# A chunked delta rule ahead of a SwiGLU block: the first pair of chunks solved with 16-row blocks and rounds u = v + N u, its loads reordered

## The chip, the cores and the metric

The kernel runs on one core of a Trainium2 chip. The metric is the device time of one execution in microseconds (us); lower is better. Five engines work side by side: TensorE (PE, matrix products into PSUM), VectorE (DVE), ScalarE (ACT), GpSimd (POOL) and SyncE (SP, which issues most loads and stores). Each takes its instructions in order.

## The reference

```python
# q, k, v: (4, 8, 768, 48); beta: (4, 8, 768); d_model 384, d_ff 1536; all float32
k_n = k / (norm(k, axis=-1) + 1e-6)
state = zeros((B, H, D, D))
for t in range(S):
    y[:, :, t] = einsum('bhd,bhde->bhe', q[:, :, t], state)
    v_old = einsum('bhde,bhd->bhe', state, k_n[:, :, t])
    state += beta[:, :, t] * outer(k_n[:, :, t], v[:, :, t] - v_old)
x = y.transpose(0, 2, 1, 3).reshape(3072, 384)
g = x @ w_gate
out = (g * sigmoid(g) * (x @ w_val)) @ w_out
```

The recurrence runs over 768 positions for each of 32 pairs of batch and head. The feed-forward network (FFN) then works on 3072 tokens.

## The kernel before

**Chunks.** The positions are cut into 12 chunks of 64 (`C`), two chunks to a group. Within a chunk the recurrence becomes a triangular system: with the strictly lower part L of diag(beta) K K^T, the updates u of all 64 positions are u = (I + L)^-1 diag(beta) (v - K state). `gram` makes the products K K^T and Q K^T on PE, `mask_q` cuts the latter to its triangle into `p_sb`. `invert` makes the inverse's diagonal blocks of 32 rows (`R`) for both chunks of a group and all heads at once: 128 partitions hold 4 blocks of 32 rows, the free dimension holds 32 x 32 elements. `substitute` runs it on DVE, 31 steps of one product (`tmp`, L524) and one addition (`zb`, L530), each step waiting for the one before. The block below the diagonal is then joined on PE (`join`, for the first two groups `join_late` with its helpers `late_z` and `d_o`), and the transposed inverse lies in `ztp`.

**One chunk's steps.** `advance(c)` is a generator with four or five steps: K state and Q state (p_r, p_y), u by the inverse (p_u, copied to `uu`), the new state (p_s) and y (p_y), then y turned by PE (p_f) into the FFN's input `x_ffn`.

**The FFN.** `gate_val(c, f)` makes 2 x 128 columns of gate and of value for the 256 tokens of chunk c (24 passes of PE at L1052; a float32 product is two passes in the profile), Silu on ACT and the product of both on DVE. From chunk 2 on a form with fewer products is used (`gate_val_fast`, L957, and `output_fast`, L1160). Between their products, `point` puts steps of the next chunks into PE's queue, and `fill` puts weight conversions or substitution steps into DVE's.

**Weights.** The 36 pieces of weights are staged by SP as raw words (`stage`, L250) into tiles that are free at that time, and `convert` brings each into its place with two activations on ACT (`power_step`, L262 and L268) and three instructions on DVE (L279, L287, L299). Pieces 0 to 11 hold 256 columns each (128 x 2 KB), pieces 12 to 23 hold 512; the last 12 are rows of `moe_w_out`. A place is staged again when its piece has been converted (`freed_by`). `need(n)` converts up to piece n before the products that read it.

**The order** is written out by hand for all engines (`manual_schedule`); the code's order is each queue's order. It begins with K of chunks 0 and 1 (SP and ACT queues), beta (POOL and SP), norms of K (POOL's power, L368), then four weight pieces, Q of chunk 0, K of chunks 2 and 3, six weight pieces, V of chunk 0, Q of chunk 1 and more weights. K, Q and V come in rows of 48 elements (192 bytes), four or eight loads to a chunk. The first group has its own order: `first_gram`, `first_diag` (diagonal blocks, L566), `first_below`, `first_scale` (L579 to L582), the 31 steps, `late_z`, two joins, and conversions of 12 pieces in between:

```python
        for n, _ in enumerate(substitute(mb, zb)):
            if n == R // 2:
                for i in range(4):
                    power_step(i)
        m_1 = turned_m(1, "ffn")
        scale_v_heads(0)
        turned(1, True, "px")
        for _ in late_z(0, zb):
            pass
```

After that the FFN of chunk 0 starts, with chunk 1's steps between its products. `turned_m` (L602) turns group 1's blocks on PE for its later inverse.

Of the kernel before, what the change touches and what calls it, by code (L numbers as in the profile page):

```python
# [13 lines left out]
C = 64  # L14
# [6 lines left out]
def kernel(  # L21
# [108 lines left out]
    def halves(x, c, bp, b):  # L130
        return x[2 * bp + b, :, c * C : (c + 1) * C, :]

    def load_k(c, dmas=(nc.sync,)):
        for n in range(2 * NB):
            bp, b = divmod(n, 2)
            dmas[n % len(dmas)].dma_start(
                out=kn_of(c)[64 * b : 64 * b + 64, bp, :, 0:D],
                in_=halves(k, c, bp, b).rearrange("h p d -> p h d"),
            )

    def load_q(c):
        for bp in range(NB):
            for b in range(2):
                nc.sync.dma_start(
                    out=qpad[c % QB][64 * b : 64 * b + 64, bp, :, 0:D],
                    in_=halves(q, c, bp, b).rearrange("h p d -> p h d"),
                )
# [28 lines left out]
    def load_v(c):  # L176
        vin[c] = work.tile([128, 2, NB, NJ, D], FP32, name="vin", bufs=2)
        for bp in range(NB):
            for b in range(2):
                src = halves(v, c, bp, b).rearrange("(j par) p d -> par p j d", par=2)  # L180
                for par in range(2):
                    s = 64 * (b ^ par)
                    nc.sync.dma_start(out=vin[c][s : s + 64, par, bp], in_=src[par])
# [11 lines left out]
    for f0, m in ((0, 256), (256, 256), (512, PIECE), (1024, PIECE)):  # L195
        for t in range(KT):
            for dst, src in ((wg_sb, moe_w_gate), (wv_sb, moe_w_val)):
                pieces.append((dst, src, t, f0, m))
# [22 lines left out]
    place_of += in_wo + in_z1 + in_wo + in_work + (in_z1 + in_work) * 3  # L221

    beta_s = places["wo"].bitcast(FP32)[:, 6 * H_ : 6 * H_ + NG * 128]
    LATE = {"zb": 0, "p_sb": 6}
# [13 lines left out]
    def stage(n):  # L238
# [11 lines left out]
        nc.sync.dma_start(  # L250
# [3 lines left out]
    def power_step(n):  # L254
# [3 lines left out]
        power = words(hp[10 + (n // 2 % 4 if n < N_HALF else (0, 2, 3, 1)[n % 4])])  # L258
# [11 lines left out]
    def convert(ns):  # L270
# [24 lines left out]
        for n in range(ns[-1] + 1, ns[-1] + 7):  # L295
            if n < min(N_HALF, len(pieces)) or ns[-1] + 3 > n < len(pieces):
                power_step(n)
# [15 lines left out]
    for b in range(2):  # L313
        rows = mask_q[64 * b : 64 * b + 64]
        nc.gpsimd.affine_select(
            out=rows,
            in_=rows,
            compare_op=ALU.is_ge,
            fill=0.0,
            base=-1,  # L320
            pattern=[[1, C]],
            channel_multiplier=-1,
        )

# [51 lines left out]
    def load_beta(at, queue=nc.gpsimd):  # L376
# [5 lines left out]
            in_=beta.rearrange("(bp b) (j par) s -> b par bp j s", b=2, par=2)[  # L382
# [13 lines left out]
    def scale_v_heads(c):  # L396
        r = vin[c].rearrange("p par bp j d -> p (par bp j) d")
        for h in range(HH):
            nc.scalar.mul(r[:, h], r[:, h], n_t[c // 2][:, c % 2, h : h + 1])

    scaled = set()

    def scale_v(c):
        scaled.add(c)
        spent.append(1.4)
        r = vin[c].rearrange("p par bp j d -> p (par bp j) d")
        n = n_t[c // 2][:, c % 2, :, None].to_broadcast([128, HH, D])
        nc.vector.tensor_tensor(out=r, in0=r, in1=n, op=ALU.mult)

    def banks(name, tag):  # L410

        if tag == "ffn":
            return [ps_ffn([128, 512], name) for _ in range(2)]
# [3 lines left out]
    def turned(c, of_q, tag=None):  # L417

        tag = tag or ("py" if of_q else "px")
# [5 lines left out]
        if c >= blocks_of[of_q][1]:  # L425
            xt_v = xt.rearrange("p (bp b j i) -> p bp j b i", bp=NB, b=2, j=NJ)
# [19 lines left out]
    def gram_steps(c, of_q, tag=None, copies=(nc.vector.tensor_copy,) * 2):  # L446

        xt = (qt if of_q else kt)[c]
        p_g = banks("p_g", tag or ("py" if of_q else "px"))
# [47 lines left out]
    z1s, mbs = {}, []  # L497
    WAIT = "wait"
# [40 lines left out]
    first_of = {}  # L539

    def first_tiles():
        a = work.tile([128, C * 2 * HH], FP32, name="a_sb")

        first_of["flat"] = a[:, 0 : R * R]
        first_of["diag"] = a[:, 0 : R * R].rearrange("p (j h) -> p h j", j=R)
        a_sb[0] = a[:, R * R :].rearrange("p (c h j) -> p c h j", c=2, h=HH)
        zb = work.tile([128, R, R], FP32, name="zb", bufs=1)
        nc.vector.memset(zb, 0.0)
        nc.vector.memset(ztp[0], 0.0)
        first_of["zb"] = zb  # L550

    def first_gram(c, tag):
# [9 lines left out]
        return p_g, p_v  # L562

    def first_diag(c, par, p, copy):
        at = HH * c + HH // 2 * par
        copy(first_of["diag"][:, at : at + HH // 2], p[1][:, par, 1])  # L566

    def first_below(c, p):
        for lo in (slice(R, C), slice(64 + R, 64 + C)):
            nc.scalar.copy(  # L570
                a_sb[0][lo, c].rearrange("p (par h) j -> p par (h j)", par=2),
                p[0][lo, :, 0 : HH // 2 * R],
            )

    def first_scale(mb, r_b):
        zb, b = first_of["zb"], beta_b[:, 0]
        nb = work.tile([128, R], FP32, name="nb", tag="nb_1", bufs=1)
        for _ in range(2):
            nc.gpsimd.tensor_tensor(out=b, in0=b, in1=r_b, op=ALU.mult)  # L579
        nc.gpsimd.tensor_copy(zb.rearrange("p k i -> p (k i)")[:, 0 : R * R : R + 1], b)  # L580
        nc.vector.tensor_scalar_mul(nb, b, -1.0)
        nc.vector.tensor_tensor(  # L582
            out=mb, in0=mb, in1=nb[:, None, :].to_broadcast([128, R, R]), op=ALU.mult
        )
        return zb
# [7 lines left out]

    def turned_m(g, tag):

        a_v = a_of[g].rearrange("p (m i) -> p m i", i=C)
        p_m = banks("p_m", tag)
        half_r = R // 2
        for j in range(R):
            p = p_m[j // half_r][:, R * (j % half_r) : R * (j % half_r) + R]  # L600
            for quad, at in QUADS:
                nc.tensor.matmul(p[quad], a_v[quad, :, at + j], ident[quad, quad])  # L602
        return [
            (slice(half_r * n, half_r * n + half_r), p.rearrange("p (j i) -> p j i", i=R))
            for n, p in enumerate(p_m)
        ]
# [50 lines left out]
    def invert(g):  # L657
# [3 lines left out]
        if g > 1:  # L661
            mb = new_mb()
            yield from turn(mb.rearrange("p j i -> p i j"), a_v[:, R:C])
        else:
            mb = mbs.pop()
# [82 lines left out]
    def advance(c):  # L748
# [7 lines left out]
        p_y = recur(ps_pair("p_y", "py"))  # L756
        if c > 0:
            p_r = recur(ps_pair("p_r", "px"))
# [20 lines left out]
        yield  # L779
        p_u = recur(ps_pair("p_u", "px"))  # L780
        for bp, j, par, b, first in every():
# [8 lines left out]
        uu = work.tile([128, 2, NB, NJ, D], FP32, name="uu", tag="r", bufs=2)  # L790
        each = range(NB) if c == 0 else (slice(0, NB),)
        for bp in each:
            nc.scalar.copy(uu[:, :, bp], p_u[:, :, bp])
# [6 lines left out]
        pq = p_sb.pop(c)  # L800

        def p_of_u():
            for bp, j, par, b, first in every():
# [4 lines left out]
                    start=(c == 0 and first),  # L808
# [29 lines left out]
        p_of_u()  # L838
        y = work.tile([128, NB, NJ, 2, D], FP32, name="y", tag="r", bufs=2)
        for bp in each:  # L840
            nc.scalar.copy(y[:, bp, :, 0], p_y[:, 0, bp])
            for b in range(2):
                nc.scalar.copy(y[half_of(b), bp, :, 1], p_y[half_of(1 - b), 1, bp])
# [201 lines left out]
    def gate_val(c, f, fill, within=None):  # L1045

        ps = {}
        for w_sb, name in ((wg_sb, "p_gate"), (wv_sb, "p_val")):
# [11 lines left out]
            if name == "p_gate":  # L1060
                nc.scalar.activation(sil, ps[name], ACTF.Silu)
                fill(2)
                if within is not None:
                    point(within)
        new_h(c, f, len(hs))
        nc.vector.tensor_tensor(out=hs[c, f], in0=sil, in1=ps["p_val"], op=ALU.mult)
        fill(3)
# [24 lines left out]
    def store(c, bp, o_sb):  # L1092
        for b in range(2):
            nc.sync.dma_start(
                out=out_v[2 * bp + b, c * C : (c + 1) * C],
# [166 lines left out]

    gens = {}

    def step(kind, fn, *args):
# [3 lines left out]
        next(gens[key][0], None)  # L1269
        gens[key][1] += 1  # L1270
# [22 lines left out]
    first = []  # L1293
# [13 lines left out]
    def may_advance(c):  # L1307
        g = c // 2
        due = {0: 1, 1: 2 + 2 * (c % 2)}.get(g, 2)
# [13 lines left out]
    def prep_step(c):  # L1323

        if first:
            first.pop(0)()
            return True
# [46 lines left out]
    def fill(n):  # L1374
        if todo:

            filled.append(n)
            converts(2 if len(filled) < 4 else 1)
            if len(filled) == 1:
                converts(1)  # L1380
# [17 lines left out]
    with tc.manual_schedule(  # L1398
# [9 lines left out]
        for at in range(0, 16, 2):  # L1408
            load_beta(at)
            load_beta(at + 1, nc.sync)  # L1410
# [3 lines left out]
        nc.vector.memset(places[0][:, 0:1], 0)  # L1414
        norms(1)
        for n in range(4):
            stage(n)
# [3 lines left out]
        for n in range(4, 10):  # L1421
            stage(n)
        load_v(0)
        load_q(1)
        stage(10)
        stage(11)
        copy_a, copy_v = nc.scalar.copy, nc.vector.tensor_copy
        turned(0, False)
# [8 lines left out]
        mb = new_mb()  # L1437
        nc.vector.transpose(
            mb.rearrange("p j i -> p (j i)"), first_of["flat"]
        )  # L1440
        for n in range(12, 17):
            stage(n)
        load_v(1)
        zb = first_scale(mb, r_b)
        for c in range(2):
            first_below(c, p_g[c])

        turned(0, True, "ffn")
        turned(2, False, "px")
        turned(3, False, "py")  # L1450
        first_q = gram_steps(0, True, "ffn")
        next(first_q)
        gram(2, False, "px", (copy_a, copy_a))
        gram(3, False, "py", (copy_a, copy_a))
        for n, _ in enumerate(substitute(mb, zb)):
            if n == R // 2:
                for i in range(4):
                    power_step(i)
        m_1 = turned_m(1, "ffn")
        scale_v_heads(0)  # L1460
# [101 lines left out]
```

## Time and profile before

| | us |
|---|---|
| median of 3 runs (713.03 to 714.13) | 713.82 |
| the profiled execution, time | 713.96 |
| its span, first to last instruction | 712.3 |
| PE busy | 679.6 |
| DVE busy | 475.6 |
| ACT busy | 261.8 |
| POOL busy | 53.8 |

A row of the profile's groups names the line, engine and operation, then output and inputs with shapes. Busy times of different engines overlap. The chain of waits goes back from the last instruction: at each step to what released it, or to the instruction before it on its engine, so its pieces add up to the span. The granted clock is the share of full speed at which PE was allowed to run.

### The profile page before, as it was taken

What the parts mean: (1) busy time and instruction counts of PE and PEld (TensorE: products, weight loads), DVE (VectorE), ACT (ScalarE), POOL (GpSimd) and SP (SyncE); (2) the same over time, 40 slices, a digit from 0 to 9 for tenths busy, and PEclk for the clock granted to TensorE, in tenths of its full rate; (3) what the DMA queues carried; (4) which work ended last, traced back from release to release, by engine and by line L of the source; (5) the groups of instructions that cost most, each with busy time, mean ns of one, the idle gap of its engine ahead of it and who ended that gap; (6) DMA issues with size and microseconds to landing.
All of it is one profiled execution on the core that took longest, in us unless ns stands there. A gap on an engine that the chain in (4) does not pass through costs nothing.

```text
span 712.3 us, 25668 instructions
## 1 busy us (share of the span) xinstructions
PE 679.6 (95%) x11368; PEld 637.9 (90%) x11368; DVE 475.6 (67%) x1085; ACT 261.8 (37%) x555; POOL 53.8 (8%) x46
## 2 busy tenths in 40 slices
PE   4747999999999999999999999999999999999997
PEld 3636788866799999999999999999999999999997
DVE  5995765779799967888458888469854345333342
ACT  3557755312453343224333235233153043142230
POOL 8003000201300030000120000300000000000000
PEclk9556999999999999999999999999999999999999
DMA  7786444002753162166144166035142142121210
GB/s 149 173 230 171 128 112 131 26 12 45 206 111 80 40 119 67 26 136 133 29 97 105 25 125 123 18 97 113 24 112 71 24 99 60 47 68 46 67 46 22
DMA packets 144575, 62.57 MB, mean 88 GB/s; under 512 B 124400, under 2 KB 127472, under 8 KB 144464
## 3 DMA queue, kind: packets, MB, share of 16 engines
q1 hardware_dynamic: 141968, 60.36, 36.1%
q8 instruction: 89, 1.46, 0.8%
q10 hardware_dynamic: 2112, 0.39, 0.4%
q0 software_dynamic: 384, 0.17, 0.1%
q14 instruction: 22, 0.18, 0.1%
HBM read 53.82 MB, written 7.08 MB: 86 GB/s over the span
## 4 chain that ended last, share of the span: by engine, by line
PE 89%; DVE 5%; ACT 3%; issue 1%; DMA 1%; SPq 0%; DVEq 0%; ACTq 0%
PE ffn L957 42%; PE ffn L1160 19%; PE ffn L1052 9%; PE ffn L1077 4%; PE p_g L452 3%; PE p_s L816 2%; PE p_r L760 2%; PE p_u L782 2%; DVE tmp L524 2%; DVE zb L530 2%; PE p_y L769 1%; PE p_y L804 1%; PE p_f L853 1%; DMA kn<-in_k_dram 1%; PE p_j L723 1%
## 5 line engine op out<-in xcount | busy, mean ns | idle before, releaser
L957 PE MATMUL ffn<-x_ffn,wg_sb 128*128 128x128 f32 x840 | 128.3, 275 | 0.4 <-ACT x_ffn L856 0.2
L957 PE MATMUL ffn<-x_ffn,wv_sb 128*128 128x128 f32 x840 | 128.1, 275 | 0.0
L957 PEld LDWEIGHTS ffn<-x_ffn,wg_sb 128*128 128x128 f32 x840 | 111.1, 192 | 0.7 <-ACT ffn L1013 0.3
L957 PEld LDWEIGHTS ffn<-x_ffn,wv_sb 128*128 128x128 f32 x840 | 110.7, 192 | 0.0
L987 ACT ACTIVATE sil<-ffn 128x256 f32<-128x256 f32 x120 | 46.0, 383 | 131.9 <-PE ffn L957 126.8
L1160 PE MATMUL ffn<-wo_sb,h_f 128*128 128x192 f32 x480 | 83.4, 327 | 0.0
L992 DVE TENSOR_TENSOR h_f<-sil,ffn 128x256 f32<-128x256 f32 x120 | 49.6, 418 | 47.6 <-ACT sil L987 45.1
L1160 PEld LDWEIGHTS ffn<-wo_sb,h_f 128*128 128x128 f32 x480 | 78.1, 190 | 0.4
L1121 DVE TENSOR_TENSOR ffn<-ffn,p_sb 128x512 f32<-128x512 f32 x58 | 40.4, 696 | 44.6 <-ACT ffn L1013 43.5
L530 DVE TENSOR_TENSOR zb<-zb,tmp 128x31 f32<-128x31 f32 (+15 forms) x186 | 63.7, 343 | 6.4
L524 DVE TENSOR_TENSOR tmp<-zb,mb 128x31 f32<-128x31 f32 (+15 forms) x186 | 63.2, 340 | 5.2
L957 PE MATMUL ffn<-x_t,h_f 128*128 128x128 f32 x480 | 61.2, 280 | 0.1
L957 PEld LDWEIGHTS ffn<-x_t,h_f 128*128 128x128 f32 x480 | 56.2, 191 | 1.4 <-ACT ffn L970 0.3
L668 POOL TENSOR_TENSOR n_b<-mb,half 128x32 f32<-128x32 f32 x5 | 30.0, 5995 | 297.6 <-DVE mb L494 258.5
L1121 DVE TENSOR_TENSOR o_sb<-o_sb,ffn 128x192 f32<-128x192 f32 x49 | 17.2, 351 | 51.2 <-PE ffn L1160 49.1
L970 ACT COPY ffn<-ffn 128x512 f32<-128x512 f32 x30 | 17.1, 571 | 63.6 <-PE ffn L957 57.2
L1052 PE MATMUL ffn<-x_ffn,wg_sb 128*128 128x256 f32 x144 | 35.8, 401 | 0.9 <-ACT x_ffn L856 0.9
L1160 PE MATMUL ffn<-last_k,h_f 128*128 128x192 f32 x200 | 35.9, 327 | 0.0
L1052 PE MATMUL ffn<-x_ffn,wv_sb 128*128 128x256 f32 x144 | 33.4, 381 | 0.0
L1052 PEld LDWEIGHTS ffn<-x_ffn,wg_sb 128*128 128x128 f32 x144 | 28.3, 201 | 5.6 <-ACT x_ffn L856 1.4
L1160 PEld LDWEIGHTS ffn<-last_k,h_f 128*128 128x128 f32 x200 | 32.9, 190 | 0.0
L1052 PEld LDWEIGHTS ffn<-x_ffn,wv_sb 128*128 128x128 f32 x144 | 27.0, 190 | 3.7
(242 smaller groups left out, 1048.1 us busy)
## 6 DMA issues: line engine op xcount, KB each, us to landing
h_f<-w_s SPq DMA_DIRECT2D x60, 256.0 KB
p_sb<-w_s SPq DMA_DIRECT2D x27, 256.0 KB
vin<-in_v_dram SPq DMA_DIRECT2D x96, 48.0 KB
out_dram<-o_sb SPq DMA_DIRECT2D x48, 96.0 KB
kn<-in_k_dram SPq DMA_DIRECT2D x40, 96.0 KB
zt<-in_moe_w_out_dram SPq DMA_DIRECT2D x6, 384.0 KB
qpad<-in_q_dram SPq DMA_DIRECT2D x36, 64.0 KB
wo_sb<-in_moe_w_gate_dram SPq DMA_DIRECT2D x4, 512.0 KB
```

The costliest lines, as they stand in the source:

```text
L452: nc.tensor.matmul(p_v[par][half_of(b if of_q else b ^ par), bp, j], kt[c][half_of(par), bp, j, b], xt[half_of(par), bp, j, b],)
L524: nc.vector.tensor_tensor(out=t_v, in0=zb[:, 0 : j + 1, j : j + 1].to_broadcast([128, j + 1, m]), in1=mb[:, j : j + 1, j + 1 : R].to_broad ...
L530: nc.vector.tensor_tensor(out=zb[:, 0 : j + 1, j + 1 : R], in0=zb[:, 0 : j + 1, j + 1 : R], in1=t_v, op=ALU.add,)
L668: nc.gpsimd.tensor_tensor(out=n, in0=mb.rearrange("p j i -> p (j i)")[:, 0 : R * R : R + 1], in1=half, op=ALU.pow,)
L957: nc.tensor.matmul(p[:, u], w(u), moving, start=start and u == 0, stop=True, skip_group_check=True,)
L970: nc.scalar.copy(p_y, p_x)
L987: nc.scalar.activation(sil[:, n].rearrange("p (i n) -> p i n", i=2), p[:, 0:2], ACTF.Silu)
L992: nc.vector.tensor_tensor(out=h_of(c, f, j), in0=sil[:, n].rearrange("p (i n) -> p i n", i=2), in1=p[:, 2:4], op=ALU.mult,)
L1052: nc.tensor.matmul(ps[name][:, i], w_sb[:, t, (f + i) * 128 : (f + i + 1) * 128], xts[c][:, t], start=(t == 0 and i == 0), stop=(t == KT - 1),
L1077: nc.tensor.matmul(p_o, hs[c, f - f % 2][:, f % 2, bp * 128 : (bp + 1) * 128], wo_sb[:, f], start=(f == 0), stop=(f == FT - 1),)
L1121: nc.vector.tensor_tensor(out=out, in0=a, in1=b, op=ALU.add)
L1160: nc.tensor.matmul(p[x, part], a(f - f % 2)[:, f % 2], b(f), start=not begun and f == 0, stop=f == FH - 1, skip_group_check=True,)
```

## The change

- The first group uses diagonal blocks of 16 rows: 15 steps on two blocks per partition (`first_substitution`) for the 31 steps on one.
- Instead of joining blocks, N = -Z L is made on PE (`n_products`, from the blocks below the diagonal in `l_sb` and the block inverse in `ztp[0]`), then v0 = Z r, and three rounds u = v0 + N u. With four blocks of 16 rows, N^4 is zero, so three rounds are exact. For chunk 0 the halves of each round (`par`) lie in PSUM tiles of their own and one weight piece is converted behind each half's addition.
- The joins, `turned_m` and the scaling of v by heads on ACT go; v of chunks 0 and 1 is scaled on DVE. The Gram product of Q and K of chunk 1 comes ahead of the FFN.
- Loads: K and Q of a chunk in two transfers, V in four; K and Q of chunks 0 to 3 and V of chunk 0 ahead of all weights; four of the beta loads on ACT's queue. The batches are assigned to the halves of the partitions the other way, in loads and stores.
- Weight columns 512 to 1023 come in pieces of 256, so there are 42 pieces; six are converted before the FFN starts, where it were twelve.
- 100 one-column products into PSUM that nothing reads, ahead of the first transposes.
- In chunk 0's first two gate blocks a step of `advance` and one or two conversions follow each quarter of the products.

```diff
+    def load_heads(t, x, c, dmas=(nc.sync,)):
+        for b in range(2):
+            dmas[b % len(dmas)].dma_start(
+                out=t[64 * b : 64 * b + 64, :, :, 0:D].rearrange("p bp h d -> p (bp h) d"),
+                in_=halves(x, c, b).rearrange("bp h p d -> p (bp h) d"),
+            )
...
-    for f0, m in ((0, 256), (256, 256), (512, PIECE), (1024, PIECE)):
+    for f0, m in ((0, 256), (256, 256), (512, 256), (768, 256), (1024, PIECE)):
...
+    def unread():
+        p = ps_pair("p_t", "px")[:, 0]
+        for n in range(100):
+            q_ = QUADS[n % 4][0]
+            nc.tensor.matmul(p[q_, 0:1], ident[q_, q_], ident[q_, 0:1])
...
+    def first_substitution():
+        zb, mb = pairs_of_blocks(first_of["zb"]), pairs_of_blocks(first_of["mb"])
+        for j in range(B16 - 1):
+            m = B16 - 1 - j
+            shape = [128, 2, m, j + 1]
...
+            nc.vector.tensor_tensor(
+                out=t_v, in0=zb[:, :, j : j + 1, 0 : j + 1].to_broadcast(shape),
+                in1=m_v.to_broadcast(shape), op=ALU.mult,
+            )
+            nc.vector.tensor_tensor(out=z_v, in0=z_v, in1=t_v, op=ALU.add)
...
+    def n_products(c, p_n, pars):
...
+                nc.tensor.matmul(
+                    p_v[par][half_of(b), bp, j], l_sb[c][rows, h], zt[rows, h]
+                )
...
     def advance(c):
...
+        if c < 2:
+            yield MORE
+            uu = new_u("uu")
+            p_n = single(2) if c == 0 else [p_u[:, par] for par in range(2)]
+            for n in range(3):
+                for par in by_par(p_n, n_sb[c], uu if n else v0, 0, True):
+                    if c == 0:
+                        plus(uu[:, par], v0[:, par], p_n[par])
+                        if n + par < 3:
+                            yield MORE
+                if c > 0:
+                    plus(uu, v0, p_u)
+                    if n < 2:
+                        yield MORE
...
-            load_beta(at + 1, nc.sync)
+            load_beta(at + 1, nc.sync if at % 4 else nc.scalar)
...
-        for n in range(4):
-            stage(n)
         load_q(0)
         load_k(2)
         load_k(3)
-        for n in range(4, 10):
+        load_q(1)
+        load_v(0)
+        for n in range(12):
             stage(n)
-        load_v(0)
-        load_q(1)
-        stage(10)
-        stage(11)
+        load_v(1)
+        stage(12)
+        stage(13)
...
+        unread()
         turned(0, False)
         turned(1, False, "py")
...
+        first_substitution()
+        for n in range(14, 18):
+            stage(n)
+        first_z()
+        for n in range(18, 23):
+            stage(n)
+        some, others = slice(0, HH // 2), slice(HH // 2, HH)
+        spread_z(0, 1, nc.scalar, some)
+        spread_z(0, 0, nc.vector)
+        spread_z(0, 1, nc.vector, others)
+        scale_v(0)
...
+        step("advance", advance, 0)
+        power_step(0)
+        power_step(2)
...
+        for n in (0, 2, 4, 1, 3, 5):
+            step("advance", advance, 0)
+            converts_first(n)
+        step("advance", advance, 0)
+        p_n = banks("p_n", "px")
+        n_products(1, p_n, (0,))
+        step("advance", advance, 0)
+        n_products(1, p_n, (1,))
+        scale_v(1)
...
+        def chain(at):
+            step("advance", advance, 0 if steps("advance", 0) < 4 else 1)
+            converts(1 + (at + 1) % 2)
```

`first_z` transposes the block inverse (1024 elements); `spread_z` copies it with a mask into `ztp[0]`, for half the rows each time; `low_copies` brings the blocks below the diagonal from PSUM to `l_sb` on ACT, 12 copies for both chunks; `n_copy` brings N from PSUM to SBUF on ACT.

## The prediction

> **What bounds the kernel now.** I read the page first, then the busy time by stretch, then the chain of waits of the first 80 us, then the order of VectorE's (DVE's) instructions. The page says that TensorE (PE) is the bound, but not in the first slices:
>
> ```profile
> PE 679.6 (95%) x11368; PEld 637.9 (90%) x11368; DVE 475.6 (67%) x1085; ACT 261.8 (37%) x555; POOL 53.8 (8%) x46
> ...
> PE   4747999999999999999999999999999999999997
> ...
> PEclk9556999999999999999999999999999999999999
> ```
>
> In the table by stretch (columns: PE, weight loads, DVE, ACT, POOL busy, clock granted to PE, DMA share, GB/s) the bound changes hands at about 80 us: until 60 DVE is busy nine tenths and PE idles at half clock, afterwards PE is full.
>
> ```profile
> 30.00:40.00 10.00, 4.32 (x256) 3.92 (x256) 9.21 (x24) 7.59 (x27) 0.00 (x0) 0.63 0.68 175
> ...
> 50.00:60.00 10.00, 6.00 (x189) 5.06 (x180) 8.64 (x29) 9.66 (x26) 3.26 (x1) 0.50 0.54 118
> 60.00:70.00 10.00, 9.05 (x150) 7.26 (x151) 4.02 (x8) 5.65 (x11) 2.37 (x1) 0.66 0.69 195
> ...
> 80.00:90.00 10.00, 10.00 (x224) 8.56 (x223) 7.01 (x11) 5.15 (x10) 0.00 (x0) 1.00 0.05 14
> ```
>
> The chain says what fills the opening (start, length, what): 31 substitution steps of two DVE instructions, then transposes, a join and its copies, then the first FFN product at 62.37, at half clock (5.03 against 2.80 us for the same 12), and a last hole that ends at 78.54.
>
> ```profile
> 20.34 0.20 DVE tmp L524
> ...
> 21.87 0.28 DVE tmp L524
> ...
> 59.87 1.55 PE p_f L853 x6
> ...
> 62.37 5.03 PE ffn L1052 x12
> 67.40 1.08 PE p_s L816 x64
> 68.48 0.68 PE ffn L634 x50
> 69.16 2.80 PE ffn L1052 x12
> ...
> 77.91 0.58 ACT zt L654
> ...
> 78.54 1.16 PE p_g L452 x64
> ```
>
> So the span is F, the start of the first FFN product, plus the PE work behind it, plus PE's losses there. Before: F = 62.4. From 78.54 on PE is full: 712.3 - 78.5 = 633.8. Between F and 78.54 PE did 12 + 12 FFN passes (5.6 at full clock), L816 (1.1), L634 (0.7) and most of L646 (1.9): 9.3 us of work in 16.2, so 6.9 were lost, 2.2 of it to the clock. Work behind F: 633.8 + 9.3 = 643.1.
>
> **Part 1, up to the substitution (ends at 20.3 before).** POOL's two powers (L368, 6.50 us from 9.20) end at 15.7, and add, reciprocal and transpose bring r_b at 16.6. These stay. Behind them the change needs the last diagonal copy (0.59), the 1024-element transpose (1.25), nb (0.14) and a scaling of 512 elements instead of 1024 (0.65 for 1.23): 19.3, if the diagonal is there. The diagonal may be the later one: four beta loads now sit in ACT's queue ahead of the first K copies, at the 0.61 us that one beta load costs SP, and they wait for earlier loads, so I put those copies at 10 rather than 7.5. PE then reaches the second Gram block at 12.5; before, it stood from 12.7 to 15.4 in an "issue" gap between records, so there is room, and I take 19.3 to 20.3, middle 19.8. The new zero fills, mask sums and products of m_rows are small DVE work ahead of 6.38, where DVE waited for K anyway; without that cover they would cost about 1 us.
>
> **The 100 unread products** (1 column each, two passes) run before K lands. The Gram products, as small, did about 208 passes from 9.84 to 12.53: 12.9 ns each. 200 passes are 2.6 us, from 2.1 to 4.7; K's first chunk starts its DVE work at 6.38, so they cost nothing. The Trainium skill ("TensorE: Matmul & The Clock Gate", "Wait — 56ns, not 53.3ns?") speaks against it: no start-to-start below about 25 ns, and 62 ns where firmware decodes. That is an estimate of 5.0 us (end at 7.1, 0.7 late) or 12.4 (end at 14.5, some 7 late). The measured 12.9 ns is already under that floor, as four quadrants take turns, so I take it. Nor do I see a gain: the clock row shows 9 for the first slice already, it falls to half at about 15.6, right behind PE's gap, 11 us after these products are done, and no stage before then is set by PE. Bounds -1 and +7, value 0.
>
> **Part 2, the substitution.** The old steps fit 0.195 us + 1.05 ns per element, start to start (31 elements 0.23, 112 elements 0.31); the fit gives 23.5 for the measured 23.4. The new one has 15 steps x 2 instructions over 1360 elements of each kind: 30 x 0.195 + 2720 x 0.00105 = 8.7 us. Saved 14.6. It ends at 28.5.
>
> **Part 3, from there to F (18.7 us before).** What goes: the transposes L610 and L616 (1.92 + 1.21), the join's copies (1.30 + 0.38 + 2.36), two copies of m (0.59 each) and six pairs of weight pieces in between; the 16 scalings of v on ACT (3.70) become one of DVE. What comes, on DVE: transpose 1.2 (L616 1.21), two spreads of 512 and 256 (0.65 + 0.4, from L582), the scaling of v (0.95, as L356), four masked copies (2.6, L470 1.29 for two): 34.3. PE meanwhile at half clock: 64 passes of N (2.2) and 64 of p_u (2.0; L804 took 1.96) from 30.8 give 35.0; ACT's copies of N (0.6 each) fit, if ACT is free by then: from 16.9 it has 12 copies of the blocks below the diagonal (5.8, by L570's 0.59 for 512 elements), 8 of K and Q (4.3) and 4 of Gram blocks (2.2), to 29.2, and its first spread comes at 29.7; 0.5 of cover, and what exceeds it delays F. The halves of v0 (0.6) are there at 35.6. Six half rounds follow. Their PE part (32 passes, 1.0) hides behind DVE, whose own sequence is one addition of 384 elements from PSUM (0.56, between 192 elements in 0.351 and 512 in 0.696) and one weight piece (0.29 + 0.42 + 0.42 + 0.1 of gaps = 1.23, when it stands alone): 1.83. First addition done at 35.6 + 1.0 + 0.7 = 37.3, the sixth at 46.4. Then p_y's second half 1.0, y copies 0.7, p_f 1.55, x copies 0.9 and gaps 0.2: F = 50.8, against 62.4: 11.6 earlier. The separate PSUM tiles are what lets one half's products run while the other half is added; without it each half round would be 1.0 longer, 6 us in all.
>
> **Part 4, behind F.** PE work: three rounds for chunk 1 (3 x 1.08) are added; its join (0.68 + 1.94) goes, and one Gram block (1.16) has moved ahead of F: -0.5, so 642.6. Losses: the cold clock again, 2.2. Only 6 weight pieces are converted at F, 12 before, and the second gate block needs 12, the third 18, the fourth 24. DVE up to there: 18 pieces at 0.86 (paired) to 1.23, about 19 (6 pieces of 512 columns are now 12 of 256: 1.72 a pair for some 1.6, nothing), and additions, state and h 8: 27 us. PE up to there: 30.6. DVE has about 4 us of cover, but ACT holds two pieces' activations (0.66 a piece) ahead of a copy that PE needs (about 1 us), and the fourth block waits for the last three pieces (about 1). 4.5 lost by this schedule, 6.9 in the old; I take 6.
>
> **The loads.** SP, ACT and POOL issue the same first loads; SP is moved past Q0, K2, K3, Q1, V0 (about 2 MB in 192-byte rows) before the first weights. Issue costs per load hardly depend on size (0.61 for 48 KB, 0.63 to 0.71 for 96 KB), so half as many loads issue faster, and the rows then run at the 130 to 200 GB/s of 2 to 8 us and 16 to 24 us: 10 to 15 us from about 8.5, when the second K chunk has landed. Six pieces (1.6 MB at the 350 GB/s of 24 to 28 us) then land by 23 to 28; ACT first reads one at 35. Cover 7 us or more; without it F moves one for one. K4 and the pieces behind it on SP wait for p_s at F + 4 and are needed at F + 22 and later.
>
> Sum: 50.8 + 642.6 + 6 = 699.4, and 1.66 outside the span (713.96 - 712.3): 701.1. The profiled run is 0.1 above the median of 713.82, so I say 701.0.
>
> **Rivals.**
> 1. A warmer clock. Before, one dense stretch at 26 to 29 bought 3.4 us of full clock. If the denser rounds do the same, N, p_u, p_y, p_f and the first gate products save 2.0 + 0.5 + 0.9 + 2.2, about 6: 695. Against: PE is only about half busy in the rounds, and at 6.00 of 10 us (50 to 60) the clock stayed at 0.50.
> 2. PE waits for its own instructions or for landings. It stood in "issue" gaps of 2.7 and up to 3.9 us (L560, L602) while loads ran; one such gap ahead of N and one near F: 705.
> 3. Slower than before: the weight pieces become the bound behind F. From 62.4 to 71.1 DVE finished three pieces of double size, idle in between for ACT, which waited for pieces not staged (SP queue held by PE and DVE). At that 2.9 us for each of 18 pieces the fourth gate block starts at F + 52 instead of F + 35 (1.9 a piece with all else): 718. It turns the sign from F + 48 on, 2.7 us a piece. Against: pieces 6 to 22 are staged before F.
> 4. The 100 products cost the estimate's long end, 7 us: 708. Against: the 12.9 ns.
>
> **How the numbers follow.** Forecast 0.60 (its own range 697 to 706), rival 1 0.16, rival 2 0.14, rival 4 0.03, rival 3 0.06, and 0.01 for one that ends at no change. 694 to 708 leaves out rival 3 and the tails. A change under 0.2% (1.4 us) can't be told from none: faster 0.93, same 0.01, slower 0.06.
>
> **What would show it.** Substitution rows 30 in 8.7 us, starting at 19 to 20; additions about 1.8 us apart; first FFN product at 49 to 53, at half clock; PE full from about F + 36. Wrong if additions lie over 2.5 us apart, if PE waits for a landing of a weight piece, or if the stretch F to F + 40 shows PE under 8 of 10.

## The result, and the profile after

The changed kernel takes 709.26 us (median of 5 runs, 706.98 to 710.56), and the kernel before, beside it on the same chip, 714.13 (713.03 to 715.15): a ratio of 0.9932, with a 95% interval of 0.9909 to 0.9956. The change gains 4.9 us, where the forecast was a gain of 13. The profiled execution took 709.14 with a span of 707.4, against a forecast span of 699.4. So 8.0 us are to be explained: F, the start of the first FFN product, came at 53.4 instead of 50.8, and the part behind it took 654.0 instead of 648.6.

The page of the changed kernel, first rows (busy time, then TensorE and its clock in 40 slices, then the queue that carries instructions: packets, MB, share):

```profile
PE 683.2 (97%) x11440; PEld 643.0 (91%) x11440; DVE 473.6 (67%) x1092; ACT 261.8 (37%) x548; POOL 52.9 (7%) x46
...
PE   6689999999999999999999999999999999999997
...
PEclk9799999999999999999999999999999999999999
...
q8 instruction: 90, 1.47, 0.9%
```

PE was busy for 679.6 us before and is so for 683.2 now; 2.8 of the 3.6 more are the unread products. The clock row has lost its stretch of fives. The last row is one that the prediction did not read: 1.47 MB in 90 packets are 16 KB a packet.

The stretches that the prediction showed; 30 to 40 is where it had put the N products (columns: PE, weight loads, DVE, ACT, POOL, clock granted to PE, DMA share, GB/s):

```profile
30.00:40.00 10.00, 4.87 (x179) 4.62 (x178) 4.57 (x8) 3.54 (x9) 0.00 (x0) 0.83 0.88 241
50.00:60.00 10.00, 9.77 (x288) 8.13 (x284) 3.95 (x11) 6.47 (x17) 0.00 (x0) 1.00 0.44 81
60.00:70.00 10.00, 9.49 (x211) 7.98 (x210) 6.52 (x16) 7.41 (x21) 0.00 (x0) 1.00 0.10 26
80.00:90.00 10.00, 9.55 (x166) 8.10 (x166) 6.09 (x20) 7.86 (x17) 0.00 (x0) 1.00 0.66 216
```

From 50 on PE is full and warm, as hoped. But from 30 to 40 every engine in the row is idle for more than half of the time. The chain of waits of the changed kernel tells what stood there (start, length, what):

```profile
29.44 0.52 PE ffn L458 x33
29.95 4.41 issue
34.36 1.02 PE ffn L458 x28
...
35.49 1.71 PE p_n L667 x62
...
40.62 0.04 DVE uu L1260
...
42.21 0.55 DVE uu L1260
...
48.56 0.56 DVE uu L1260
...
53.46 0.63 PE ffn L1189 x2
```

PE stops in the middle of Q1's Gram products, after 33 passes, and the row names no other engine that it waited for. That its next instructions were missing is what experiments 4 to 7 and 11 go into. The N products, queued behind, begin at 35.1 instead of 31. The six additions (L1260) are then 1.6 us apart.

### The profile page after: what moved, and what is told of

Read it like the earlier page. It is cut to its first block, busy times and chain, and to the rows that moved or that the text cites. A ratio compares the mean times of both kernels' runs of the same rounds, so it can differ in the third digit from the quotient of the medians.

```text
span 707.4 us, 25711 instructions
## 1 busy us (share of the span) xinstructions
PE 683.2 (97%) x11440; PEld 643.0 (91%) x11440; DVE 473.6 (67%) x1092; ACT 261.8 (37%) x548; POOL 52.9 (7%) x46
## 3 DMA queue, kind: packets, MB, share of 16 engines
q8 instruction: 90, 1.47, 0.9%
## 4 chain that ended last, share of the span: by engine, by line
PE 91%; DVE 3%; ACT 2%; issue 2%; DMA 1%; SPq 0%; DVEq 0%; ACTq 0%
PE ffn L1093 42%; PE ffn L1299 19%; PE ffn L1189 8%; PE ffn L1216 4%; PE p_g L458 3%; PE p_u L876 2%; PE p_s L944 2%; PE p_r L838 2%; PE p_y L932 1%; PE p_y L847 1%; DMA kn<-in_k_dram 1%; PE p_f L989 1%; PE p_u L896 1%; PE p_t L444 1%; PE p_j L801 1%
## 5 line engine op out<-in xcount | busy, mean ns | idle before, releaser
L1093 PEld LDWEIGHTS ffn<-x_ffn,wg_sb 128*128 128x128 f32 x840 | 111.1, 192 | 0.7 <-ACT ffn L1149 0.3
L1260 DVE TENSOR_TENSOR ffn<-ffn,p_sb 128x512 f32<-128x512 f32 x58 | 40.4, 697 | 44.3 <-ACT ffn L1149 43.2
L536 DVE TENSOR_TENSOR zb<-zb,tmp 128x31 f32<-128x31 f32 (+15 forms) x155 | 53.1, 343 | 5.3
L530 DVE TENSOR_TENSOR tmp<-zb,mb 128x31 f32<-128x31 f32 (+15 forms) x155 | 52.7, 340 | 4.0
L1260 DVE TENSOR_TENSOR o_sb<-o_sb,ffn 128x192 f32<-128x192 f32 x49 | 17.2, 352 | 51.2 <-PE ffn L1299 49.1
L1189 PE MATMUL ffn<-x_ffn,wg_sb 128*128 128x256 f32 x144 | 34.3, 384 | 0.0
L1093 PE MATMUL ffn<-x_ffn,p_sb 128*128 128x128 f32 x216 | 30.3, 283 | 0.5 <-issue 0.5
```

The source lines that it names most:

```text
L530: nc.vector.tensor_tensor(out=t_v, in0=zb[:, 0 : j + 1, j : j + 1].to_broadcast([128, j + 1, m]), in1=mb[:, j : j + 1, j + 1 : R].to_broad ...
L536: nc.vector.tensor_tensor(out=zb[:, 0 : j + 1, j + 1 : R], in0=zb[:, 0 : j + 1, j + 1 : R], in1=t_v, op=ALU.add,)
L1093: nc.tensor.matmul(p[:, u], w(u), moving, start=start and u == 0, stop=True, skip_group_check=True,)
L1189: nc.tensor.matmul(ps[name][:, i], w_sb[:, t, (f + i) * 128 : (f + i + 1) * 128], xts[c][:, t], start=(t == 0 and i == 0), stop=(t == KT - 1),
L1260: nc.vector.tensor_tensor(out=out, in0=a, in1=b, op=ALU.add)
```

## The experiments

Each was timed beside the kernel before. "F" and "behind F" are of the profiled execution.

| kernel | median us (range) | ratio to before (95%) | F | behind F |
|---|---|---|---|---|
| the change | 709.26 (706.98 to 710.56) | 0.9932 (0.9909 to 0.9956) | 53.4 | 654.0 |
| 1: no unread products | 705.28 (705.13 to 708.72) | 0.9881 (0.9866 to 0.9897) | 52.4 | 651.5 |
| 2: chunk 1's rounds on four quadrants | 706.24 (705.84 to 708.97) | 0.9897 (0.9882 to 0.9911) | 53.0 | 651.2 |
| 3: same order, two quadrants | 708.6 (706.65 to 708.98) | 0.9913 (0.9900 to 0.9925) | 54.4 | 652.9 |
| 4: some weights later | 709.32 (705.40 to 711.47) | 0.9917 (0.9890 to 0.9943) | 53.0 | 654.5 |
| 5: 64 unread products | 706.73 (704.20 to 708.91) | 0.9907 (0.9894 to 0.9921) | 50.7 | 651.8 |
| 6: 36 unread products | 706.71 (705.20 to 708.71) | 0.9901 (0.9886 to 0.9916) | 50.8 | 653.9 |
| 7: 128 unread products | 712.28 (708.67 to 713.40) | 0.9963 (0.9951 to 0.9975) | 59.1 | 651.3 |
| 8: as 1 and 4 together | 707.26 (705.92 to 709.41) | 0.9908 (0.9894 to 0.9922) | 56.4 | 651.2 |
| 9: loads paced | 709.20 (706.65 to 713.08) | 0.9933 (0.9908 to 0.9958) | 51.5 | 653.5 |
| 10: as 1 and 9 together | 706.50 (705.54 to 707.14) | 0.9889 (0.9876 to 0.9902) | 54.0 | 651.3 |
| 11: 36 unread products behind F | 710.70 (708.93 to 711.42) | 0.9939 (0.9926 to 0.9951) | 55.0 | 654.7 |

Two habits help with this table. The part behind F repeats well: experiments 1, 5, 7, 8 and 10, which will turn out to be alike there, give 651.2 to 651.8. F does not: less the 651.5 behind it, the five spans of experiment 1 (703.4 to 707.0) give an F from 51.9 to 55.5. Experiment 11 executes the same instructions as 1 up to F, and its profile has F 2.6 us later. So F of one profile is one draw, and for what happens ahead of F the medians are the measure.

**1. Without the unread products.** The call is left out.

```diff
-        unread()
```

> The changed kernel without its 100 unread products. Theory A (they do nothing for the time): PE's granted clock in 27 to 60 us stays at full speed as in the changed kernel, the first FFN product starts within 1.5 us of 53.5 apart from where PE's gaps of its own instructions fall (400 records fewer, so the gap of 4.4 us at 30 us moves), and the time lies at 706 to 710. Theory B (they keep the clock up for the first stage): the clock falls to half in most of 10 to 50 us as it did before the change, the first FFN products take 0.42 us a pass instead of 0.25, the first FFN product starts 2 to 4 us later, and the time is 711 to 714.

The median fell to 705.28, 4 us under the change, with intervals that do not touch. It lies under the ranges of both theories. Theory B is right in part, as the opening has more of the half clock without the products: granted at half from 16.9 to 23.7 and from 33.9 to 44.2 us, against 20.8 to 27.6 and 34.4 to 37.8 in the change. But the kernel is faster all the same, and its first six FFN passes take 1.49 us, at full clock, as in the change.

The products' own time is not the reason, for in the change they ran at about the speed that the prediction took from the Gram products (14.2 ns a pass against 12.9). The start of PE's timeline of the changed kernel:

```profile
1.90 2.84 PE L582 MATMUL p_t<-ident 32*32 32x1 f32 x200 [1.90 <-POOL ident masks.py:199]
5.85 1.94 PE L444 MATMUL p_t<-ident,kn 128*128 128x128 f32 x8 [1.11 <-DMA kn<-in_k_dram]
```

200 passes from 1.90 to 4.74, and then PE waits for K anyway. The Trainium skill's floors of 25 or 62 ns ("TensorE: Matmul & The Clock Gate", "Wait — 56ns, not 53.3ns?") did not hold for them, and yet the products were not free. What they take is not time but places: 100 products are 400 instructions (two passes, each with its weight load). Experiments 5 to 7 and 11 follow that.

**2 and 3. Chunk 1's rounds.** They took 2.0 us each instead of the 1.08 in the prediction's sum. In the change, head half b goes from rows b to output rows b, so only the two diagonal 64 x 64 quadrants of the array are used. Experiment 2 takes the order of the other products and sends the odd heads to the other half, so that all four quadrants take turns (it serves to measure only, as these heads' values are then not the reference's); 3 keeps that order but stays on the diagonal.

```diff
-                for par in by_par(p_n, n_sb[c], uu if n else v0, 0, True):
+                if c > 0:
+                    for bp, j, par, b, first in every():
+                        nc.tensor.matmul(
+                            p_n[par][half_of(b ^ par), bp, j],   # 3: half_of(b)
+                            n_sb[c][half_of(b), par, bp, j],
+                            (uu if n else v0)[half_of(b), par, bp, j],
...
```

> Rounds of chunk 1 in the order of the p_u products, with the odd heads' results written to the other half of the partitions: the same 64 passes a round, but over all four 64 x 64 quadrants of PE instead of the two on the diagonal. The odd heads' values of chunk 1 are thereby not the reference's. Theory A (two quadrants make a round 2.0 us): each of the three rounds takes 1.1 us, the span falls by up to 2.8 us if DVE does not then set the pace, time 706.5 to 708. Rival (the round is slow because it waits for the additions or because of its PSUM tile): the rounds stay at 2.0 us and the time at 709.

> Rounds of chunk 1 in the order of the p_u products (odd and even heads mixed), each still on the diagonal quadrants; the result is the reference's. Theory A (the quadrants, not the order): a round stays at 2.0 us, time 709. Rival (the order of heads and of PSUM banks): 1.1 to 1.4 us a round and 706.5 to 708.

PE's timeline of experiment 2, then of 3 (two rounds and the FFN batch between them):

```profile
63.72 1.15 PE L913 MATMUL p_u<-v,zb 64*64 64x48 f32 x64 [0.49 <-ACT v L888]
64.80 1.56 PE L1199 MATMUL ffn<-x_ffn,wg_sb 128*128 128x256 f32 x6
66.29 1.15 PE L913 MATMUL p_u<-uu,zb 64*64 64x48 f32 x64
```

```profile
65.06 2.07 PE L913 MATMUL p_u<-v,zb 64*64 64x48 f32 x64 [0.33 <-ACT v L888]
67.06 1.56 PE L1199 MATMUL ffn<-x_ffn,wg_sb 128*128 128x256 f32 x6
68.55 2.07 PE L913 MATMUL p_u<-uu,zb 64*64 64x48 f32 x64
```

From start to next start a round is 1.08 us on four quadrants (16.9 ns a pass) and 2.00 on two (31 ns). The part behind F falls by 2.8 (654.0 to 651.2), which is three times 0.92. Against experiment 3 it falls by 1.7 only, as 3's trace has 0.8 us less of the holes that experiments 5 to 7 are about. Order alone changes nothing about a round: edits 2 and 3 differ in the output half alone. So the quadrants are the cause of the 2.0 us, and this is shown. It fits what the Trainium skill says ("TensorEngine Tiling (Array Packing)", "Key Properties"), that such tiles work independently of each other.

**4. Weight pieces later.** The hole at 30 ends 2.4 us after the start of a 16 KB packet on the instruction queue, at 32.0. The two holes before it, at 13 and 17 us, are about 1 us each. SP had issued twelve weight pieces of 256 KB from 22.7 to 29.2. Here six of them and V of chunk 1 go behind pieces 18 to 22.

```diff
-        for n in range(12):
+        for n in range(6):
             stage(n)
-        load_v(1)
-        stage(12)
-        stage(13)
...
         for n in range(18, 23):
             stage(n)
+        for n in range(6, 12):
+            stage(n)
+        load_v(1)
+        stage(12)
+        stage(13)
```

> Weight pieces 6 to 13 and V of chunk 1 are issued after the pieces that wait for the block inverse, so that little is in flight from 27.5 to 28.4 us. Theory A (the gap of 4.4 us at 30 us is PE's fetch of its next 16 KB of instructions, held up behind load packets): the fetch starts by 29.5 instead of 32.0, the gap falls to under 2 us, the first FFN product starts at 50 to 51.5, and, if the late pieces are in time, the time is 705 to 707. Rival (the gap is a fixed cost of a fetch, or comes from something else on PE): gap 4 us or more, time 709 or above.

PE's timeline of experiment 4, then of experiment 2:

```profile
31.30 0.74 PE L458 MATMUL ffn<-qt,kt 64*64 64x64 f32 x28 [2.80 <-issue]
...
37.01 0.68 PE L876 MATMUL p_u<-vin,zt 64*64 64x48 f32 x32 [2.33 <-issue]
```

```profile
30.26 0.63 PE L458 MATMUL ffn<-qt,kt 64*64 64x64 f32 x28 [2.27 <-issue]
...
36.44 1.10 PE L876 MATMUL p_u<-vin,zt 64*64 64x48 f32 x32 [3.44 <-issue]
```

The packet came at 28.8 instead of 32.0, and the hole shrank from 4.4 to 2.8 us, but a second one of 2.3 us opened, F came at 53.0 and not by 51.5, and the median did not move. Nor can the shorter hole be credited to the later loads. Experiments 2 and 3 have the same opening as the change, loads included. In their traces this packet starts at 27.8 and 29.9, while the 2 KB rows of the weights run on until about 33, the hole is 2.3 and 3.2 us, and the second hole is there too (3.4 and 3.6). So 28.8 lies within what the unchanged opening draws.

**5 to 7. Other numbers of unread products.** In all traces here PE's holes of over 2 us that are marked "issue" begin exactly behind instruction 449, 705, 961 and so on, in steps of 256 (16,384 bytes, 64 each), where products, weight loads and the records of PE's sequencer are counted. The two of the kernel before that the prediction quotes, 2.7 and 3.9 us, stand behind 449 and 1473, and the 4.41 of the change behind 1473 too. 64 and 128 products are one and two whole steps.

```diff
-        for n in range(100):
+        for n in range(64):    # 6: range(36), 7: range(128)
```

> The change with 64 unread products in place of 100: 256 records of TensorE (two passes, each with its weight load), which is exactly one of the pieces in which TensorE's instructions arrive; the pieces then end at the same instructions as with none. Theory A (what the products cost is where they shift the ends of the pieces to): about 705.5, as with none; F near 52.5, no gap over 3 us ahead of the N products. Theory B (they cost by their number, through work and records): about 707.8, 64 hundredths of the 4.0 us that 100 cost.

> 36 unread products, 144 records: 400 less 256, so the pieces end at the same instructions as with 100. Theory A: as with 100, about 709.3, with the hole of 4 us in the Gram products of Q1 at about 30. Theory B: about 706.7.

> 128 unread products, 512 records, two whole pieces. Theory A: 705.5, or up to 0.7 more where the products, now 3.4 us long, end at about 7.2 and so hold up the first transposes of K. Theory B: 710.4.

Neither theory holds in all three totals: 36 products come out as their number has it (706.71), 64 lie between the two (706.73), 128 above both (712.28). Experiment 6 has the hole in Q1's Gram products that theory A put there, but of 2.7 us and at 26. Cut at F, each has its part. Behind F, place alone decides: none, 64 and 128 products give 651.5, 651.8 and 651.3; 36 and 100 give 653.9 and 654.0. The difference arises at PE's holes. They are these five in the changed kernel, and the last four of them in experiment 6 too; none is there with 0, 64 or 128. From PE's timeline of the changed kernel:

```profile
169.59 0.26 PE L838 MATMUL p_r<-state,kt 64*64 64x48 f32 x2 [0.38 <-issue]
...
173.97 0.33 PE L876 MATMUL p_u<-vin,zt 64*64 64x48 f32 x6 [0.55 <-issue]
...
177.97 0.43 PE L932 MATMUL p_y<-uu,p_sb 64*64 64x48 f32 x10 [0.30 <-issue]
...
257.25 0.27 PE L815 MATMUL p_j<-t,z 32*32 32x32 f32 x9 [0.89 <-issue]
...
354.94 1.05 PE L1093 MATMUL ffn<-x_ffn,p_sb 128*128 128x128 f32 x7 [0.53 <-issue]
```

Every one stands at a multiple of 256 instructions from the 449th; together they are 2.65 us. Without the products there is one such hole instead, 0.96 us at F + 23. Set product against product from F on, the change loses 3.9 us to experiment 1 at its five holes, gains 1.2 at that one and 0.2 later, which makes the 2.5.

Ahead of F nothing so clear is to be had. Less the part behind F and the 1.7 outside the span, the medians of 0, 36, 64, 100 and 128 products put F at 52, 51, 53, 54 and 59, and experiment 11, whose opening is that of experiment 1, at 54. So only 128 stand out, and there the trace shows how. The start of PE's timeline of experiment 7:

```profile
1.90 3.16 PE L582 MATMUL p_t<-ident 32*32 32x1 f32 x223 [1.90 <-POOL ident masks.py:199]
9.63 0.60 PE L582 MATMUL p_t<-ident 32*32 32x1 f32 x33 [4.58 <-issue]
10.32 3.67 PE L444 MATMUL p_t<-ident,kn 128*128 128x128 f32 x16
```

The first 449 instructions are there at the start. The products use them up, the next ones arrive after 4.6 us, in the time in which K and Q are loaded, and K's transposes start at 10.3 instead of 5.85. F comes at 59.1. With 100 products 400 of the 449 are spent on them, but the hole of 2.8 us that experiment 1 has behind instruction 449 is then gone, and others stand elsewhere. That 100 cost anything ahead of F is not shown.

**8. Both.** Experiment 4 without the products.

> No unread products, and weight pieces 6 to 13 and V of chunk 1 issued behind pieces 18 to 22. With none of the products the fetch ahead of the N products started at 31.6 and PE stood for 1.0 and 1.9 us there. If loads in the rings are what holds a fetch up, that hole shrinks by 1 to 2 us and F comes to 51.5: 704.3. If it is the place of the pieces' ends alone, 705.3 as without the delay.

Neither expectation held: 707.26, and in its profile holes of 3.5 us at 28.2 and 3.1 us at 40.3, the latter with its packet at 41.0.

**9 and 10. Loads paced.** Pieces 6 to 11 are issued by ACT, one behind each half round; 18 to 22, 12 to 17 and V of chunk 1 by SP, where 18 has to wait. Experiment 10 leaves out the products as well.

```diff
-        for n in range(12):
+        for n in range(6):
             stage(n)
-        load_v(1)
-        stage(12)
-        stage(13)
...
-        for n in range(14, 18):
-            stage(n)
         first_z()
-        for n in range(18, 23):
+        for n in (18, 19, 20, 21, 22, 12, 13, 14, 15, 16, 17):
             stage(n)
+        load_v(1)
...
             converts_first(n)
+            stage({0: 6, 2: 7, 4: 8, 1: 9, 3: 10, 5: 11}[n], nc.scalar)
```

> The change with the same loads at other times: SP issues weight pieces 0 to 5, then 18 to 22 (which wait for the first of v's copies), 12 to 17 and V of chunk 1; ACT issues pieces 6 to 11, one behind each of the six half rounds. Between about 27 and 37 us no load is issued. Theory A (TensorE's next instructions are late because their packets stand behind a row of loads): the hole of 4.4 us at 30 falls to 1.5 us or less and F comes to 50 to 51.5; the loads behind it may hold up fetches or conversions later, so 706 to 710 in all. Theory B (the fetch is late for another reason than loads): the hole stays at 3 to 4.5 us, F 53 to 55, about 709 to 711.

> The same pacing without the 100 unread products. Theory A: F 49.5 to 51, 703 to 706. Theory B: as without the pacing, F 52.5, about 705.3.

PE's timeline of experiment 9:

```profile
27.51 0.69 PE L458 MATMUL ffn<-qt,kt 64*64 64x64 f32 x33
31.70 0.63 PE L458 MATMUL ffn<-qt,kt 64*64 64x64 f32 x28 [3.50 <-issue]
...
35.41 0.68 PE L876 MATMUL p_u<-vin,zt 64*64 64x48 f32 x32 [1.63 <-issue]
```

The hole stands behind the same 33 passes and is 3.5 us long, as theory B had it; F (51.5) is near theory A's range, and the total fits both. The packet came at 29.3, again between the 27.8 and 29.9 of experiments 2 and 3, and the second hole, of 1.6 us, is at the same instruction as theirs. So neither 4 nor 9 shows that a row of loads sets when the packet comes. The medians are those without the pacing: 709.20 against the change's 709.26, and 706.50 in experiment 10 against 705.28, with intervals that overlap.

What these edits can't settle, a count over all 13 traces narrows down. They hold 1147 steps of 256. At 80 of them PE stands for over 0.25 us with no engine named, and at 79 of the 80 the DMA engines had been over 40% busy in the 4 us before; of the 516 steps with less traffic one has such a hole, of 0.27 us. Fast work of PE alone does not explain it: of the steps whose 256 instructions PE used up in under 3 us, 39 of 73 have a hole with that traffic, 1 of 37 without. And nowhere does PE pass a step sooner than 2.2 us after its packet starts. So the 4.41 us of the change are 2.0 before the packet starts and 2.4 behind that, 1.0 of them the packet's own. This is a count and not an experiment: holes go with traffic, but which loads hold a packet up stays open.

**11. 36 products behind F.** Nothing in the opening differs from experiment 1; behind F, 144 instructions are put in. (The trace has them at 127.8 us, 73 behind F and not 30.)

```diff
-        unread()
...
-        for n in range(100):
+        for n in range(36):
...
             early = c == 0 and f < 4
+            if at == 10:
+                unread()
```

> No unread products in the opening, 36 of them behind F (ahead of the product that now starts some 30 us after F): 144 records, so that all later pieces of TensorE's instructions end where they end with 100 in front. If the holes behind F are a matter of where the pieces end: holes of 0.3 to 1.2 us come up near F + 116 to 124, F + 203 and F + 301, which are not there without the products, and the part behind F is 651.5 + 0.9 of work + 1.7 to 2.6 = 654 to 655, about 708 in all. If those holes come from the opening: 652.4 behind F, 706.2 in all.

The part behind F is 654.7, in the range of the first theory, and three of the holes are back, at the same instructions. Of the 3.2 us over experiment 1's 651.5, 1.0 arises at the products themselves. (The total is higher than expected because F came late, at 55.0.) PE's timeline of experiment 11:

```profile
180.21 0.43 PE L932 MATMUL p_y<-uu,p_sb 64*64 64x48 f32 x10 [0.30 <-issue]
...
259.50 0.27 PE L815 MATMUL p_j<-t,z 32*32 32x32 f32 x9 [0.62 <-issue]
...
357.17 1.05 PE L1093 MATMUL ffn<-x_ffn,p_sb 128*128 128x128 f32 x7 [0.47 <-issue]
```

So the holes behind F belong to the place of the steps, whatever the opening did.

The lowest median is that of experiment 1, the change without its unread products: 705.28 us, 1.2% under the kernel before.

## Why the prediction was wrong

The direction was right, the sum was not. Three of its terms failed: PE's wait for its own instructions ahead of the N products, put at nothing; the rounds of chunk 1, mis-sized; and the work behind F, miscounted. The 8.0 us by the prediction's own steps, F first and then the part behind it:

- **Part 3, to F: +2.6.** The prediction had the first addition start at 36.6; it started at 40.62, 4.0 late, because of the hole of 4.4 us. This is rival 2, which the prediction named and gave 0.14, with one gap ahead of N, one near F, and 705 in all. Part of it came back: the additions were 1.59 us apart and not 1.83, as the addition and the three steps of a weight piece (0.56 + 0.29 + 0.42 + 0.42 = 1.69 by their rows) overlap a little, where the sum had gaps. The sum itself has no term for this wait: the part on loads looks at landings of data alone, though the holes before the change, of 2.7 and 3.9 us, were marked "issue" in the same way.
- **Part 4, the rounds of chunk 1: +2.8.** "Three rounds for chunk 1 (3 x 1.08)" was costed by rows that use four quadrants. The code says `flip` 0 there, which leaves two. This is shown by experiments 2 and 3.
- **The work behind F before: +2.8.** It was counted from the chain of waits, which between 72 and 78.5 runs over ACT. PE did a third batch of 12 FFN passes there, which only PE's timeline of the kernel before shows:

```profile
75.30 2.86 PE L1052 MATMUL ffn<-x_ffn,wg_sb 128*128 128x256 f32 x12
```

  So 12.1 us of the 16.2 were work and only 4.1 lost, 2.2 of them to the clock. The forecast, which put 6 us of losses behind F where it saw 6.9 before, thus took 2.8 us of work for losses. This one is a matter of counting and needed no run.
- **The losses behind F: -0.2.** By the same bookkeeping (645.9 of work, less 0.5, plus 2.8) 5.8 us were lost, against 6 forecast. The size was right, its make-up was not. Nothing went to a cold clock: the first six FFN passes took 1.49 us, as rival 1 would have it, since PE's granted clock is full from 37.8 on. The holes at the steps of 256, which the prediction did not know of, took that place with 2.65.
- **Right.** The substitution began at 19.69 (forecast 19.3 to 20.3) and took 8.7 us for its 30 instructions. PE waited for the landing of no weight piece, and the pieces did not become the bound (rival 3). PE was busy for 38.9 of the 40 us behind F. The 100 products took 2.8 us (forecast 2.6) and hid behind K's load. (Two small sums do not come out, 14.6 for 23.4 - 8.7 and 4.5 for 2.2 and twice about 1; neither enters the total as such.)
- **The 100 products "cost nothing": wrong by 2.5 us behind F**, though not as rival 4 had it. This lies within the terms above and is not added to them. The other 1.5 us by which experiment 1 is faster lie ahead of F, where two kernels with the same opening (1 and 11) differ by 2, so they are not shown to be the products'.

What stays open is what holds a packet up and how much of F's spread is its doing. Runs of one kernel differ by 1.6 to 6.4 us here, where the kernel before stays within 2.4, and no order of the loads that was tried made them agree or moved the hole clear of what experiments 2 and 3 draw without any reordering. That F could be had without any hole is not shown.

## What to carry to other kernels

Where the trace says "issue" for a busy PE ahead of a stretch full of loads, count instructions to the next step of 256 before adding any, even such as take no time: they decide which work stands when the next packet is late. Before crediting an edit with a shorter hole, look at traces that share the opening without the edit. Before costing a small product by a neighbour's row, check that both use the same quadrants of the array. And count an engine's work in a stretch from its own timeline, not from the chain, which leaves out what runs beside it.

## What the runs showed of the hardware

- **Instructions come in packets, and a late packet stops PE.** The 22,880 matmuls and weight loads of the change, behind the first 449, are 87.6 steps of 256, near the page's 90 packets of 16 KB. A packet takes 0.9 to 2.0 us in these traces, PE passes its step no sooner than 2.2 us after its start, and the longest hole is 4.6 us. The Trainium skill ("Runtime: NRT & Kernel Launch", "Instruction fetch mechanics") gives the same step, 256 instructions, and calls the crossing "mostly hidden". It is hidden at most of the crossings here, and costs 0.3 to 1.1 us at seven of them and 4.41 at one in the changed kernel.
- **Holes go with traffic.** 79 of the 80 holes of over 0.25 us at such steps, in these traces, stand where the DMA engines had been over 40% busy.
- **Places matter, not only numbers.** 36 idle products, less than 1 us of work, put in 73 us behind F cost 3.2 us behind it (654.7 against 651.5).
- **Two quadrants cost nearly twice as much as four**: 31 against 16.9 ns a pass for 64 x 48 products in fp32.
